# Two heads of lookahead in an attention search, fewer plain products and moved clamps in an attention + MoE kernel

## The chip, the cores and the metric

The kernel runs on one core of one Trainium2 chip. The metric is device microseconds of that core for one execution; the time of a kernel is the median of its runs. The profile shows one further execution.

## What is computed

```python
def reference(q, k, v, moe_*, moe2_*):             # B, H, S, D = 2, 8, 576, 64
    scores = matmul(q, k^T) / sqrt(D)              # float32 everywhere below
    kth = 32nd largest of each row                 # np.partition
    scores = where(scores >= kth, scores, -1e9)
    attn = softmax(scores)                         # sum + 1e-9 in the divisor
    x = (attn @ v) -> (1152 tokens, 512)
    x = ((x @ w_a) * (x @ w_b)) @ w_out            # MoE 1, 512 -> 1536 -> 512, weights float64
    p = domain_probs / (sum + 1e-9)                # MoE 2, 4 experts, 512 -> 1024 -> 512
    return sum_e p[:, e] * (relu(x @ w1[e]) @ w2[e])
```

## The kernel before

Every product is made in two parts, high and low (fp32r), by three passes: the high part is a copy to fp32r (ACT), the low part a subtraction (`split_sb`, L294 and L295, POOL or DVE). The exceptions are "plain" fp32 products: the scores of the (head, batch) pairs in `PLAIN`, which are all (h, 0), and group 0's product with v ("native").

The 1152 tokens are 9 tiles of 128, in three groups of 3 tiles; group 0 takes tiles 3 to 5, which lie in both batches. For each group come the attention of 8 heads x 3 tiles, MoE 1 (`pa`, `pb`, `px`), and MoE 2 (`ph`, `po`).

*Group 0's attention* (called stage 1 below): head by head, `prep(h)` loads q and k (`load_qk`) and splits them; `scores` makes a tile's scores on TensorE (PE) and ACT copies them to `Sb`; in the same step the scores of that head for groups 1 and 2 are made too and kept in DRAM (`stash`, names `pk`, `keep`). DVE then searches each row for its 32nd largest: four MAX8 and three MATCH_REPLACE8 that depend on each other (`top`, `W`, L210 and L212), so the scheduler interleaves two tiles. POOL (group 0) or DVE makes `nm`, ACT the masked exponential in two passes (`Ex`, L218 and L219), PE transposes it (`PT`, `PL`), ACT copies it (`Ph`). `finish(h)`, called in the step after the head's last tile, is the product with v (`pO`), and for every second head the scaling `rs`, `rb`, `pR`, `xf` (L244 to L269), then the split `x`.

*Decode stage*: w_a, w_b and w_out are 18 units of 128 x 1024 numbers in float64. Each is loaded (`wide`, 2 x 512 KB), decoded to float32 (ACT L315, a clamp on POOL L317, ACT L322, two DVE operations L324 and L325 per half), stored to DRAM for the later groups (`da`, `db`, `do`) and split. The first three units are gated by the exponentials and the searches of the last three tiles of group 0 (`GATE`), the others by the last one. Group 0's MoE 1 products follow the units.

*After that* group 0's MoE 2 runs with the attention of group 1 among it, then group 1's MoE with group 2's attention, then group 2's MoE. The order of steps is set by a table of paces, and a scheduler then orders instructions on each engine; each engine runs its own in order.

Buffers in rings: `Sb` 9 (shared with `keep`), `gh` 8, `big` 7, `w` 5, `wraw` 3, `ps_s` 2.

Of the kernel before, what the change touches and what calls it, by code (L numbers as in the profile page):

```python
# [9 lines left out]
F32 = mybir.dt.float32  # L10
R32 = mybir.dt.float32r
# [9 lines left out]
P = 128  # L21
# [8 lines left out]
NB2 = S // P + 1  # L30
N0 = H * GROUPS[0]

NX, NW, NH, NR, NB = 5, 5, 8, 3, 7
NWK, NS, NE, NV = 2, 9, 2, 3
# [17 lines left out]
WC = 256  # L52
# [3 lines left out]
def f32(ap):  # L56
    return ap.bitcast(F32)
# [3 lines left out]
def kernel_body(ctx, tc, qs, ks, vs, wa, wb, wo, dp, w1, w2, out):  # L61
# [43 lines left out]
    kept = {}  # L105
    parts = [[(b, t - b * (S // P)) for b in range(B) if b * S < (t + 1) * P and (b + 1) * S > t * P] for t in range(NT // P)]

    def load_qk(h):
        for b in range(B):
            n = f"{h}_{b}"  # L110
            sl = slice(b * NB2, (b + 1) * NB2)
            kr = sb.tile([P, 4 * WC], F32, tag="big", name=f"kr{n}", bufs=NB)[:, :S]
            qr = sb.tile([P, 2 * MT], F32, tag="gh", name=f"qr{n}", bufs=NH)[:, :NB2 * P].rearrange("p (t c) -> p t c", t=NB2)
# [31 lines left out]
    def attention_steps(g):  # L145
        tpg = GROUPS[g]
        gt = tpg * P
        bt = batches(g)
        native = g in NATIVE
        st = {}  # L150

        def prep(h):
            n = f"{g}_{h}"
            V = {}
            if h % 2 == 0:
                st["sums"] = at.tile([P, MG, 2, 1], F32, tag="sums", name=f"sums{n}")
                st["x"] = at.tile([P, MT], F32, tag="xf", name=f"xf{n}")[:, :gt]
            PL = ps_t.tile([P, 512], F32, tag="PL", name=f"PL{n}")
            Pe = at.tile([P, MT], R32, tag="Pe", name=f"Pe{n}")
            Ph = at.tile([P, 4, MT], R32, tag="Ph", name=f"Ph{n}")  # L160
            Pl = None
            if g == 0:
                load_qk(h)
            if native:
                for b, _, _ in bt:
                    V[b] = at.tile([P, KC, D], F32, tag="V2", name=f"V2{n}_{b}", bufs=NV)
                    nc.sync.dma_start(V[b], vs[b, h])
                Ph, Pe = f32(Ph), f32(Pe)
            else:
                for b, _, _ in bt:  # L170
                    vr = at.tile([P, KC, D], F32, tag="vraw", name=f"vraw{n}_{b}", bufs=1)
                    nc.sync.dma_start(vr, vs[b, h])
                    V2 = at.tile([P, KC, 2 * D], R32, tag="V2", name=f"V2{n}_{b}", bufs=NV)
                    o = D * (h % 2)
                    nc.scalar.activation(V2[:, :, o:o + D], vr, AF.Copy)
# [9 lines left out]
                st["S", i] = S1  # L185

        def scores(h, t):
            if g:
                return st.pop(("S", h * tpg + t))
# [6 lines left out]
            for i in range(1, NG):  # L196
                stash(i, h, t)
            return Sb

        def one_tile(h, t):  # L200


            n = f"{g}_{h}_{t}"
            V, Ph, Pl, Pe, PL, sums, _ = st[h]
            Sb = scores(h, t)
            top = at.tile([P, 32], F32, tag="top", name=f"top{n}")
            W = at.tile([P, S], F32, tag="W", name=f"W{n}", bufs=NWK)
            src = Sb
            for r in range(4):
                last["max", g, h * tpg + t] = nc.vector.max(top[:, 8 * r:8 * r + 8], src).ins  # L210
# [17 lines left out]
                nc.vector.tensor_tensor(Pl[:, :, cols], PT, f32(Ph[:, :, cols]), op=ALU.subtract)  # L228

        def close(h):  # L230
            V, Ph, Pl, Pe, PL, _, _ = st[h]
            nc.scalar.activation(Pe[:64, :gt], PL[:64, :gt], AF.Copy)
            if not native:
                nc.vector.tensor_tensor(Pe[64:, :gt], PL[:64, :gt], f32(Pe[:64, :gt]), op=ALU.subtract)

        def finish(h):
            n = f"{g}_{h}"
            V, Ph, Pl, Pe, PL, sums, xf = st.pop(h)
            late = h == H - 1
            if h % 2:  # L240
# [55 lines left out]


    nload = [0]
    scratch = {}

    def decode(raw, src, n):

        half = 2 * WC
        words = src.bitcast(U32).rearrange("p (n t) -> p n t", t=2)
        gate = GATE[min(len(scratch), len(GATE) - 1)]
        r = raw.bitcast(U32)
        wide = []
        with tc.issue_after(last["exp", 0, gate]):  # L310
# [73 lines left out]
    def moe_steps(g):  # L384
# [159 lines left out]
```

## Time and profile before

| | |
|---|---|
| runs | 922.59, 946.72, 939.25 us; median 939.25 |
| profiled execution | 923.0 us, span 921.2 us, 1.8 us around it |
| mean granted clock of TensorE | 0.970 |
| busy | PE 848.6 us (92%), PEld 744.8, DVE 608.4 (66%), ACT 523.3 (57%), POOL 467.8 (51%) |
| HBM traffic | 141.75 MB, mean 154 GB/s |

The busy shares are means over stages with different limits: PE is nearly full from some 340 us to the end and has gaps before that, while DVE is nearly full from some 160 to 340 us and again from some 480 to 600 us, and four tenths busy or less after that.

### The profile page before, as it was taken

Reading aid. Unit: us, or ns where it says so; the run is one execution under the profiler, and the core shown is the slowest. Engines: PE = TensorE matmul, PEld = TensorE weight load, DVE = VectorE, ACT = ScalarE, POOL = GpSimd, SP = SyncE. Lnnn points to the kernel's source line nnn. Section 1 sums busy time; section 2 is a strip of 40 time slices with the busy share of each in tenths; the row PEclk is TensorE's granted clock in tenths of the full one; section 3 lists DMA queues with packets and bytes.
Section 4 is the critical chain, followed back from the end, with each engine's and each line's share of the span. In section 5 each row is a group of like instructions: output and inputs, shape, how many; then the busy total and the mean of one; then the engine's idle time right before and its main releaser. Section 6 shows DMA issues by size and latency. Waiting matters only on the chain.

```text
span 921.2 us, 12500 instructions
## 1 busy us (share of the span) xinstructions
PE 848.6 (92%) x4332; PEld 744.8 (81%) x4332; DVE 608.4 (66%) x1171; ACT 523.3 (57%) x948; POOL 467.8 (51%) x265
## 2 busy tenths in 40 slices
PE   7988979567777999999999998999999999999997
PEld 5655545357677889999999998999989999899997
DVE  5679587999999997588589999932123222423332
ACT  5776767678777766455567776553333444343330
POOL 4321100579889875545657575455553535422330
PEclk9999988779998999999999999999999999999999
DMA  9645426488765654444455442324334442433420
GB/s 258 197 163 182 147 90 217 132 254 259 239 236 192 205 185 135 140 160 127 152 172 170 140 153 84 115 95 134 128 124 150 136 135 95 153 121 119 139 85 35
DMA packets 50304, 141.75 MB, mean 154 GB/s; under 512 B 5824, under 2 KB 9920, under 8 KB 50240
## 3 DMA queue, kind: packets, MB, share of 16 engines
q1 hardware_dynamic: 50240, 140.94, 47.0%
q8 instruction: 34, 0.56, 0.2%
q14 instruction: 30, 0.25, 0.1%
HBM read 114.97 MB, written 25.95 MB: 153 GB/s over the span
## 4 chain that ended last, share of the span: by engine, by line
PE 62%; DVE 10%; issue 2%; DMA 2%; ACT 0%; DVEq 0%; SPq 0%; ACTq 0%
PE po L451 21%; PE ph L381 20%; PE pb L381 5%; PE pa L381 5%; PE px L420 5%; DVE top L210 2%; DVE W L212 2%; PE PT L223 2%; DVE x L295 1%; PE pO L259 1%; PE pO L258 1%; DVE wraw0o L325 1%; DVE Pl L228 1%; DMA do<-wraw0o 1%; DMA da<-wraw0a 0%
## 5 line engine op out<-in xcount | busy, mean ns | idle before, releaser
L210 DVE MAX8 top<-W 128x8 f32<-128x576 f32 x216 | 158.9, 750 | 1.3
L438 DVE SCALAR_TENSOR_TENSOR h<-ph,h 128x384 fp32r<-128x384 f32 x96 | 52.8, 552 | 141.2 <-ACT h L437 141.1
L437 ACT ACTIVATE h<-ph 128x384 fp32r<-128x384 f32 x96 | 46.6, 489 | 117.9 <-PE ph L381 117.9
L212 DVE MATCH_REPLACE8 W<-top,W 128x576 f32<-128x576 f32 x144 | 106.8, 742 | 0.1
L451 PE MATMUL po<-w1d,h 128*128 128x512 f32 x288 | 71.0, 393 | 2.9 <-DVE xf L269 1.6
L381 PE MATMUL ph<-x,w0u 128*128 128x384 f32 x384 | 72.8, 338 | 0.3 <-DVE x L295 0.3
L381 PE MATMUL ph<-x,w1u 128*128 128x384 f32 x384 | 72.7, 337 | 0.0
L451 PE MATMUL po<-w0d,h 128*128 128x512 f32 x288 | 71.0, 394 | 0.0
L381 PE MATMUL ph<-x,w2u 128*128 128x384 f32 x384 | 70.9, 335 | 0.2 <-DVE x L295 0.2
L451 PE MATMUL po<-w2d,h 128*128 128x512 f32 x288 | 69.9, 392 | 0.0
L223 PE MATMUL PT<-ident,Ex 128*128 128x128 f32 x288 | 48.1, 290 | 23.1 <-ACT Ex L219 21.2
L381 PEld LDWEIGHTS ph<-x,w2u 128*128 128x128 f32 x384 | 67.5, 188 | 2.4 <-DVE x L295 0.5
L381 PEld LDWEIGHTS ph<-x,w0u 128*128 128x128 f32 x384 | 67.2, 188 | 2.3 <-DVE x L295 0.6
L381 PEld LDWEIGHTS ph<-x,w1u 128*128 128x128 f32 x384 | 67.4, 188 | 1.8
L210 DVE MAX8 top<-Sb 128x8 f32<-128x576 f32 x72 | 54.1, 752 | 20.7 <-ACT Ex L218 12.5
L218 ACT ACTIVATE Ex<-Sb,top 128x576 f32<-128x576 f32 x72 | 55.9, 776 | 20.2 <-DVE top L210 19.6
L451 PEld LDWEIGHTS po<-w1d,h 128*128 128x128 f32 x288 | 53.4, 188 | 13.4 <-issue 2.0
L223 PEld LDWEIGHTS PT<-ident,Ex 128*128 128x128 f32 x288 | 36.0, 147 | 34.1 <-ACT Ex L219 25.5
L451 PEld LDWEIGHTS po<-w2d,h 128*128 128x128 f32 x288 | 53.6, 188 | 10.3 <-ACT h L437 0.2
L451 PEld LDWEIGHTS po<-w0d,h 128*128 128x128 f32 x288 | 53.1, 188 | 10.0
L219 ACT ACTIVATE Ex<-Ex,nm 128x576 f32<-128x576 f32 x72 | 55.9, 777 | 7.9 <-DVE nm L215 3.8
L295 POOL TENSOR_TENSOR w1d<-wraw1d,w1d 128x1024 fp32r<-128x1024 f32 x16 | 38.7, 2424 | 38.1 <-ACT w1d L294 38.1
(140 smaller groups left out, 1976.1 us busy)
## 6 DMA issues: line engine op xcount, KB each, us to landing
k<-keep SPq DMA_DIRECT2D x48, 288.0 KB, 3.4
Sb<-k SPq DMA_DIRECT2D x48, 288.0 KB, 3.2
wraw0u<-in_w SPq DMA_DIRECT2D x16, 512.0 KB, 4.1
wraw0d<-in_w SPq DMA_DIRECT2D x16, 512.0 KB, 3.2
wraw1u<-in_w SPq DMA_DIRECT2D x16, 512.0 KB, 3.2
wraw1d<-in_w SPq DMA_DIRECT2D x16, 512.0 KB, 3.2
wraw2u<-in_w SPq DMA_DIRECT2D x16, 512.0 KB, 3.2
wraw2d<-in_w SPq DMA_DIRECT2D x16, 512.0 KB, 3.3
```

The lines of the kernel that those rows point to most:

```text
L210: last["max", g, h * tpg + t] = nc.vector.max(top[:, 8 * r:8 * r + 8], src).ins
L212: nc.vector.match_replace(W, top[:, 8 * r:8 * r + 8], src, LOW)
L218: nc.scalar.activation(Ex, Sb, AF.Prelu, bias=top[:, 31:32], scale=-1.0, alpha=KEEP)
L219: last["exp", g, h * tpg + t] = nc.scalar.activation(Ex, Ex, AF.Exp, bias=nm, scale=-1.0 / (KEEP * math.sqrt(D)), accum_out=sums[:, t, h % ...
L223: nc.tensor.transpose(PT[:, c, :], Ex[:, c * P:(c + 1) * P], ident)
L228: nc.vector.tensor_tensor(Pl[:, :, cols], PT, f32(Ph[:, :, cols]), op=ALU.subtract)
L295: eng.tensor_tensor(dst[:, 1], src, f32(dst[:, 0]), op=ALU.subtract)
L381: nc.tensor.matmul(ps, w[:, a].rearrange("p (c f) -> p c f", c=4)[:, c, col:col + P], xs[c][:, b], start=c == 0 and i == 0, stop=c == k - ...
L420: nc.tensor.matmul(p[:, :gt], w[:, a, o:o + P], ab[:, b], start=f == 0 and i == 0, stop=f == 5 and i == 2)
L437: nc.scalar.activation(ht[:, 0], p[:, :gt], AF.Relu)
L438: nc.vector.scalar_tensor_tensor(ht[:, 1], p[:, :gt], 0.0, f32(ht[:, 0]), op0=ALU.max, op1=ALU.subtract)
L451: nc.tensor.matmul(p, hs[f][:, a, t * P:(t + 1) * P], us[f // 2][:, b, (f % 2) * 512:(f % 2) * 512 + 512], start=hf == 0 and f == 0 and i ...
```

## The change

- **Plain products**: only (0, 0) stays plain. The other 15 pairs are split; for heads 1 to 7 both high parts are made by POOL copies (`CAST`), where ACT made them before. The q and k parts lie in other rings (`gh`, `big`, and a cycle of seven places for `kk`).
- **Order in stage 1**: loads three heads ahead, split and scores two heads ahead (`AHEAD`); `finish(h - 1)` and the `stash` of a tile come after the tile's own search is written. In the order that results, a pair's `xf` on DVE stands several search operations later.
- **Gate**: the first search operation of group 1's first six tiles is issued after the last decoding operation written by then (`NGATE`).
- **Clamps**: the first three units' clamp stays on POOL, the other 15 are two DVE operations each.
- **Smaller moves**: one of MoE 2's two x splits on DVE goes to POOL (`X2_DVE`), and every third low part of group 0's `h` is made by an extra ACT Relu and a POOL subtraction in place of a DVE operation (`H_POOL`).

```diff
-PLAIN = [(h, 0) for h in range(H)]
+PLAIN = [(0, 0)]
+QK_ACT = 1
+LOADS = 3
+AHEAD = 2
-GATE = (N0 - 3, N0 - 2, N0 - 1)
+CLAMP_POOL = range(3)
+GATE = (-3, -2) + (-1,) * 20
-X2_DVE = 2
+X2_DVE = 1
+H_POOL = 3
+NGATE = 6
...
+    def split_qk(h):
+        for b in range(B):
...
+            kr, qr = raw_qk[h, b]
+            A = sb.tile([P, 4 * WC], R32, tag="big", name=f"qa{n}", bufs=NB)[:, :NB2 * P].rearrange("p (t c) -> p t c", t=NB2)
+            i = nkk[0] % (NW + 2)
+            nkk[0] += 1
+            if i < NW:
+                kk = sb.tile([P, 2, 4 * WC], R32, tag="w", name=f"kk{n}", bufs=NW)
...
+            if h < QK_ACT:
+                nc.scalar.activation(A, qr, AF.Copy)
+                nc.scalar.activation(kk[:, 0], kr, AF.Copy)
+            else:
+                nc.gpsimd.tensor_copy(A, qr)
+                nc.gpsimd.tensor_copy(kk[:, 0], kr)
             nc.gpsimd.tensor_tensor(A[64:], qr[64:], f32(A[64:]), op=ALU.subtract)
+            nc.gpsimd.tensor_tensor(kk[:, 1], kr, f32(kk[:, 0]), op=ALU.subtract)
...
+                with ExitStack() as order:
+                    if r == 0 and g == 1 and h * tpg + t < NGATE and "decode" in last:
+                        order.enter_context(tc.issue_after(last["decode"]))
+                    last["max", g, h * tpg + t] = nc.vector.max(top[:, 8 * r:8 * r + 8], src).ins
...
+                    elif t == 0:
+                        for j in range(0 if h == 0 else LOADS, LOADS + 1):
+                            if h + j < H:
+                                load_qk(h + j)
+                        if h == 0:
+                            for j in range(AHEAD):
+                                split_qk(j)
+                                for u in range(tpg):
+                                    scores(j, u)
+                        if h + AHEAD < H:
+                            split_qk(h + AHEAD)
+                    if g == 0 and h + AHEAD < H:
+                        scores(h + AHEAD, t)
+                    if t == 0:
+                        prep(h)
                     one_tile(h, t)
                     if h and t == 0:
                         finish(h - 1)
+                    if g == 0:
+                        for u in range(1, NG):
+                            stash(u, h, t)
...
-        nc.gpsimd.tensor_scalar(raw, raw, -F64_TOP, F64_TOP, op0=ALU.max, op1=ALU.min)
+        if k in CLAMP_POOL:
+            nc.gpsimd.tensor_scalar(raw, raw, -F64_TOP, F64_TOP, op0=ALU.max, op1=ALU.min)
...
+                if k not in CLAMP_POOL:
+                    nc.vector.tensor_scalar(raw[:, hs], raw[:, hs], -F64_TOP, F64_TOP, op0=ALU.max, op1=ALU.min)
...
+                    if g == 0 and H_POOL and nh[0] % H_POOL == 0:
+                        hf32 = sb.tile([P, MT], F32, tag="a", name=f"hf{n}")[:, :gt]
+                        nc.scalar.activation(hf32, p[:, :gt], AF.Relu)
+                        nc.gpsimd.tensor_tensor(ht[:, 1], hf32, f32(ht[:, 0]), op=ALU.subtract)
```

On DVE, at the end of the first pair of heads in stage 1 (names are group, head, tile; `rs`, `xf` belong to the pair of heads 0 and 1), before:

```order
L244 TENSOR_SCALAR rs0_1_520<-sums0_0_81 128x6
L210 MAX top0_2_0_499<-W0_2_0_500 128x8
L245 RECIPROCAL rs0_1_520<-rs0_1_520 128x6
L269 TENSOR_TENSOR xf0_0_82<-pR0_1_525,xf0_0_82 128x384
L210 MAX top0_2_1_576<-Sb0_2_1_545 128x8
L212 MATCH_REPLACE W0_2_1_577<-top0_2_1_576,Sb0_2_1_545 128x576
```

and after:

```order
L253 MAX top0_2_0_613<-W0_2_0_614 128x8
L290 RECIPROCAL rs0_1_634<-rs0_1_634 128x6
L253 MAX top0_2_1_694<-W0_2_1_695 128x8
L255 MATCH_REPLACE W0_2_0_614<-top0_2_0_613,W0_2_0_614 128x576
L255 MATCH_REPLACE W0_2_1_695<-top0_2_1_694,W0_2_1_695 128x576
L253 MAX top0_2_0_613<-W0_2_0_614 128x8
L253 MAX top0_2_1_694<-W0_2_1_695 128x8
L255 MATCH_REPLACE W0_2_1_695<-top0_2_1_694,W0_2_1_695 128x576
L253 MAX top0_2_1_694<-W0_2_1_695 128x8
L314 TENSOR_TENSOR xf0_0_211<-pR0_1_639,xf0_0_211 128x384
L253 MAX top0_2_2_746<-Sb0_2_2_314 128x8
```

Seven search operations of the next head's first two tiles now stand between the reciprocal and `xf`, where none stood.

On PE, early in stage 1 (`pS` are scores for the search, `pk` scores to be kept, `PT` a tile's transposes), before:

```order
L132 MATMUL pS0_0_2_1_209<-kk0_1_97,qa0_1_94 128x288 x2
L132 MATMUL pk2_0_1_1_177<-kk0_1_97,qa0_1_94 128x288 x2
L132 MATMUL pk1_0_2_0_214<-kr0_0_86,qr0_0_87 128x288
L132 MATMUL pk1_0_2_1_217<-kr0_0_86,qr0_0_87 128x288
L132 MATMUL pS0_1_0_0_287<-kr1_0_268,qr1_0_269 128x288
L132 MATMUL pS0_1_0_1_290<-kr1_0_268,qr1_0_269 128x288
L223 MATMUL PT0_0_0_145<-ident_75,Ex0_0_0_142 128x128 x4
L225 MATMUL PL0_0_83<-ident_75,Ex0_0_0_142 64x128
L132 MATMUL pk2_0_2_0_223<-kk0_1_97,qa0_1_94 128x288 x2
L132 MATMUL pk2_0_2_1_227<-kk0_1_97,qa0_1_94 128x288 x2
```

and after:

```order
L268 MATMUL PL0_0_212<-ident_75,Ex0_0_0_230 64x128
L176 MATMUL pS0_1_1_0_168<-kk1_0_147,qa1_0_146 128x288 x2
L176 MATMUL pS0_1_1_1_174<-kk1_0_147,qa1_0_146 128x288 x2
L176 MATMUL pS0_1_1_0_168<-kk1_1_153,qa1_1_152 128x288 x2
L176 MATMUL pS0_1_1_1_174<-kk1_1_153,qa1_1_152 128x288 x2
L266 MATMUL PT0_0_1_287<-ident_75,Ex0_0_1_284 128x128 x4
L268 MATMUL PL0_0_212<-ident_75,Ex0_0_1_284 64x128
L176 MATMUL pS0_1_2_0_181<-kk1_1_153,qa1_1_152 128x288 x2
L176 MATMUL pS0_1_2_1_185<-kk1_1_153,qa1_1_152 128x288 x2
L299 MATMUL pO0_0_432<-Ph0_0_214,V20_0_0_215 64x192 x4
L176 MATMUL pS0_2_0_0_202<-kk2_0_190,qa2_0_189 128x288 x2
```

The scores of heads 1 and 2 now stand among head 0's transposes and ahead of most of head 0's kept scores.

On DVE, where group 0's search ends and decoding begins (`t0a`, `wraw0a` are decoding operations; `top1`, `W1` group 1's search), before:

```order
L212 MATCH_REPLACE W1_0_0_1939<-top1_0_0_1938,W1_0_0_1939 128x576
L212 MATCH_REPLACE W1_0_1_2213<-top1_0_1_2212,W1_0_1_2213 128x576
L246 COPY rb0_7_1599<-rs0_7_1598 128x384
L210 MAX top1_0_0_1938<-W1_0_0_1939 128x8
L210 MAX top1_0_1_2212<-W1_0_1_2213 128x8
L324 SCALAR_TENSOR_TENSOR t0a0_0_1631<-wraw0a0_1623,t0a0_0_1631 128x512
L215 TENSOR_SCALAR nm1_0_0_1947<-top1_0_0_1938 128x1
L212 MATCH_REPLACE W1_0_1_2213<-top1_0_1_2212,W1_0_1_2213 128x576
L325 SCALAR_TENSOR_TENSOR wraw0a0_1623<-wide0a0_0_1624,t0a0_0_1631 128x512
L210 MAX top1_0_2_2448<-Sb1_2_1934 128x8
```

and after:

```order
L396 SCALAR_TENSOR_TENSOR t0b0_0_1764<-wraw0b0_1756,t0b0_0_1764 128x512
L314 TENSOR_TENSOR xf0_6_1398<-pR0_7_1715,xf0_6_1398 128x384
L397 SCALAR_TENSOR_TENSOR wraw0b0_1756<-wide0b0_0_1757,t0b0_0_1764 128x512
L356 TENSOR_TENSOR x0_7_1732<-xf0_6_1398,x0_7_1732 128x384
L396 SCALAR_TENSOR_TENSOR t0b0_1_1768<-wraw0b0_1756,t0b0_1_1768 128x512
L396 SCALAR_TENSOR_TENSOR t0a1_0_1785<-wraw0a1_1777,t0a1_0_1785 128x512
L397 SCALAR_TENSOR_TENSOR wraw0b0_1756<-wide0b0_1_1760,t0b0_1_1768 128x512
L395 TENSOR_SCALAR wraw0b1_1798<-wraw0b1_1798 128x512
L397 SCALAR_TENSOR_TENSOR wraw0a1_1777<-wide0a1_0_1778,t0a1_0_1785 128x512
L395 TENSOR_SCALAR wraw0b1_1798<-wraw0b1_1798 128x512
L396 SCALAR_TENSOR_TENSOR t0a1_1_1789<-wraw0a1_1777,t0a1_1_1789 128x512
L397 SCALAR_TENSOR_TENSOR wraw0a1_1777<-wide0a1_1_1781,t0a1_1_1789 128x512
```

Group 1's search operations are gone from this place (the first stands some 30 rows further down), and two clamps (L395) stand per unit.

## Rows read from the trace of the kernel before

**Rows 1.** Cores: span and mean granted clock of TensorE.

```profile
core 0: 921.2 us, clock 0.970
```

**Rows 2.** Timeline of DVE in stage 1: start, us, operation, idle time before.

```profile
9.35 0.75 DVE L210 MAX8 top<-Sb 128x8 f32<-128x576 f32 x1
...
61.66 0.76 DVE L210 MAX8 top<-Sb 128x8 f32<-128x576 f32 x1 [2.23 <-ACT Sb L195]
...
99.17 0.56 DVE L269 TENSOR_TENSOR xf<-pR,xf 128x384 f32<-128x384 f32 x1 [4.90 <-ACT xf L264]
102.45 0.76 DVE L210 MAX8 top<-Sb 128x8 f32<-128x576 f32 x1 [2.73 <-ACT Sb L195]
...
175.35 1.41 DVE L210 MAX8 top<-W 128x8 f32<-128x576 f32 x2
```

**Rows 3.** Waits of DVE from 0 to 172 us: total us, times, longest.

```profile
DVE top L210 <- ACT Ex L218: 12.5, 6, 4.1
```

**Rows 4.** Timeline of PE where the stages begin: MoE 1 of group 0.

```profile
187.94 1.01 PE L381 MATMUL pa<-x,w0a 128*128 128x384 f32 x2
```

**Rows 5.** Timeline of PE: MoE 2 of group 0 begins.

```profile
320.19 2.62 PE L381 MATMUL ph<-x,w0u 128*128 128x384 f32 x14
```

**Rows 6.** Timeline of PE: group 1's MoE begins.

```profile
469.92 2.26 PE L381 MATMUL pa<-x,w1a 128*128 128x384 f32 x12
```

**Rows 7.** Windows: busy us (count) of PE, PEld, DVE, ACT, POOL, then clock, DMA share, GB/s.

```profile
20.00:40.00 20.00, 20.00 (x61) 13.54 (x61) 13.69 (x28) 14.10 (x36) 7.50 (x8) 1.00 0.63 207
200.00:220.00 20.00, 15.97 (x90) 14.46 (x88) 19.94 (x41) 17.27 (x32) 20.00 (x9) 1.00 0.85 275
...
340.00:360.00 20.00, 20.00 (x105) 18.12 (x104) 17.07 (x38) 10.36 (x18) 12.45 (x6) 1.00 0.48 156
```

**Rows 8.** The chain of waits in the decode stage: start, us, what.

```profile
309.73 5.25 DMA do<-wraw0o
```

**Rows 9.** Lines by form, DVE, 188 to 320 us: busy us, mean ns of one.

```profile
L210 DVE MAX8 top<-Sb 128x8 f32<-128x576 f32 x14 | 10.5, 750 | 0.0
```

**Rows 10.** Lines by form, POOL: busy us, mean ns, idle before.

```profile
L295 POOL TENSOR_TENSOR w0d<-wraw0d,w0d 128x1024 fp32r<-128x1024 f32 x16 | 38.7, 2424 | 32.5 <-ACT w0d L294 32.5
...
L317 POOL TENSOR_SCALAR wraw0a<-wraw0a 128x1024 f32<-128x1024 f32 x6 | 21.8, 3634 | 4.1 <-ACT wraw0a L315 4.0
...
L295 POOL TENSOR_TENSOR kk<-kr,kk 128x576 fp32r<-128x576 f32 x8 | 11.3, 1415 | 17.8 <-ACT kk L294 17.1 <-POOL qa L123 0.7
...
L246 POOL COPY rb<-rs 128x384 f32<-128x384 f32 x9 | 4.6, 508 | 2.1 <-DMA vraw<-in_v 2.1
```

**Rows 11.** Lines by form, DVE: the same columns.

```profile
L438 DVE SCALAR_TENSOR_TENSOR h<-ph,h 128x384 fp32r<-128x384 f32 x96 | 52.8, 552 | 141.2 <-ACT h L437 141.1
...
L324 DVE SCALAR_TENSOR_TENSOR t0a<-wraw0a,t0a 128x512 uint32<-128x512 uint32 x12 | 8.2, 683 | 0.0
...
L246 DVE COPY rb<-rs 128x384 f32<-128x384 f32 x3 | 1.0, 348 | 0.0
```

**Rows 12.** Timeline of POOL, 222 to 234 us.

```profile
227.91 2.41 POOL L295 TENSOR_TENSOR w0o<-wraw0o,w0o 128x1024 fp32r<-128x1024 f32 x1
```

**Rows 13.** Timeline of DVE, 225 to 233 us.

```profile
228.16 3.20 DVE L244 TENSOR_SCALAR rs<-sums 128x6 f32<-128x6 f32 x1
```

**Rows 14.** Timeline of PE, scores in stage 1, split (`kk`) and plain (`kr`).

```profile
29.89 1.16 PE L132 MATMUL pk<-kk,qa 128*128 128x288 f32 x4
...
107.87 0.69 PE L132 MATMUL pk<-kk,qa 128*128 128x288 f32 x4
...
109.63 1.23 PE L132 MATMUL pk<-kr,qr 64*128 64x288 f32 x4
```

**Rows 15.** Lines by form, PE, 320 to 470 us: the same columns.

```profile
L223 PE MATMUL PT<-ident,Ex 128*128 128x128 f32 x52 | 8.3, 274 | 1.2 <-DVE Pl L228 1.2
```

**Rows 16.** Lines by form, PE, 0 to 172 us: the same columns.

```profile
L254 PE MATMUL pO<-Ph,V 128*64 128x192 f32 x112 | 27.7, 404 | 1.8 <-ACT Ph L226 1.8
```

More of the change, by code (lines that the diff above doesn't have):

```diff
@@ L31 @@
 N0 = H * GROUPS[0]
-NX, NW, NH, NR, NB = 5, 5, 8, 3, 7
-NWK, NS, NE, NV = 2, 9, 2, 3
-PLAIN = [(h, 0) for h in range(H)]
-GATE = (N0 - 3, N0 - 2, N0 - 1)
+NX = 5
+NW = 5
+NH = 8
+NR = 3
+NB = 7
+NWK = 2
+NS = 9
+NE = 2
+NV = 3
+PLAIN = [(0, 0)]
[4 more added lines that the diff above has]
+GATE = (-3, -2) + (-1,) * 20
 W_DVE = (0, 0, 2)
-X2_DVE = 2
+X2_DVE = 1
 LOOK = 4
+H_POOL = 3
+NGATE = 6
 PRE = 4
@@ L106, in kernel_body @@
     parts = [[(b, t - b * (S // P)) for b in range(B) if b * S < (t + 1) * P and (b + 1) * S > t * P] for t in range(NT // P)]
+    raw_qk = {}
+    nkk = [0]
     def load_qk(h):
@@ L111, in load_qk @@
             sl = slice(b * NB2, (b + 1) * NB2)
-            kr = sb.tile([P, 4 * WC], F32, tag="big", name=f"kr{n}", bufs=NB)[:, :S]
-            qr = sb.tile([P, 2 * MT], F32, tag="gh", name=f"qr{n}", bufs=NH)[:, :NB2 * P].rearrange("p (t c) -> p t c", t=NB2)
+            raw = lambda c: sb.tile([P, 4 * WC], F32, tag="wraw", name=f"{c}{n}", bufs=NR) if (h, b) in PLAIN else \
+                sb.tile([P, 2 * MT], F32, tag="gh", name=f"{c}{n}", bufs=NH)
+            kr = raw("kr")[:, :S]
+            qr = raw("qr")[:, :NB2 * P].rearrange("p (t c) -> p t c", t=NB2)
             if (h, b) in PLAIN:
@@ L120, in load_qk @@
             nc.sync.dma_start(qr, qs[h, :, sl])
-            A = sb.tile([P, 2 * MT], R32, tag="gh", name=f"qa{n}", bufs=NH)[:, :NB2 * P].rearrange("p (t c) -> p t c", t=NB2)
-            nc.scalar.activation(A, qr, AF.Copy)
+            raw_qk[h, b] = kr, qr
+    def split_qk(h):
+        for b in range(B):
+            if (h, b) in PLAIN:
+                continue
+            n = f"{h}_{b}"
+            kr, qr = raw_qk[h, b]
[4 more added lines that the diff above has]
+                kk = sb.tile([P, 2, 4 * WC], R32, tag="w", name=f"kk{n}", bufs=NW)
+            elif i == NW:
+                kk = at.tile([P, 4, MT], R32, tag="Pl", name=f"kk{n}", bufs=1).rearrange("p (a b) c -> p a (b c)", a=2)
+            else:
+                kk = sb.tile([P, 4, MT], R32, tag="x2f", name=f"kk{n}", bufs=1).rearrange("p (a b) c -> p a (b c)", a=2)
+            kk = kk[:, :, :S]
+            if h < QK_ACT:
+                nc.scalar.activation(A, qr, AF.Copy)
+                nc.scalar.activation(kk[:, 0], kr, AF.Copy)
+            else:
+                nc.gpsimd.tensor_copy(A, qr)
+                nc.gpsimd.tensor_copy(kk[:, 0], kr)
             nc.gpsimd.tensor_tensor(A[64:], qr[64:], f32(A[64:]), op=ALU.subtract)
-            kk = sb.tile([P, 2, 4 * WC], R32, tag="w", name=f"kk{n}", bufs=NW)[:, :, :S]
-            split_sb(kk, kr)
+            nc.gpsimd.tensor_tensor(kk[:, 1], kr, f32(kk[:, 0]), op=ALU.subtract)
             QK[h, b] = (A, (kk[:, 0], kk[:, 1]))
@@ L148, in attention_steps @@
         bt = batches(g)
-        native = g in NATIVE
+        plain = lambda h: g in NATIVE
         st = {}
@@ L161, in prep @@
             Pl = None
-            if g == 0:
-                load_qk(h)
+            native = plain(h)
             if native:
@@ L187, in scores @@
         def scores(h, t):
-            if g:
-                return st.pop(("S", h * tpg + t))
             n = f"{g}_{h}_{t}"
@@ L195, in scores @@
                 nc.scalar.activation(Sb[:, j * SH:(j + 1) * SH], pS[:, :SH], AF.Copy)
-            for i in range(1, NG):
-                stash(i, h, t)
-            return Sb
+            st["S", h * tpg + t] = Sb
         def one_tile(h, t):
             n = f"{g}_{h}_{t}"
+            native = plain(h)
             V, Ph, Pl, Pe, PL, sums, _ = st[h]
-            Sb = scores(h, t)
+            Sb = st.pop(("S", h * tpg + t))
             top = at.tile([P, 32], F32, tag="top", name=f"top{n}")
@@ L230, in close @@
         def close(h):
+            native = plain(h)
             V, Ph, Pl, Pe, PL, _, _ = st[h]
@@ L237, in finish @@
             n = f"{g}_{h}"
+            native = plain(h)
             V, Ph, Pl, Pe, PL, sums, xf = st.pop(h)
@@ L298, in kernel_body @@
     nload = [0]
+    nh = [0]
     scratch = {}
@@ L306, in decode, with behind @@
         words = src.bitcast(U32).rearrange("p (n t) -> p n t", t=2)
-        gate = GATE[min(len(scratch), len(GATE) - 1)]
+        k = len(scratch)
         r = raw.bitcast(U32)
         wide = []
-        with tc.issue_after(last["exp", 0, gate]):
+        def behind(what):
+            gate = ExitStack()
+            if k < len(GATE):
+                gate.enter_context(tc.issue_after(last[what, 0, N0 + GATE[k]]))
+            return gate
+        with behind("exp"):
             for i in range(2):
@@ L320, in decode @@
             t = ps_s.tile([P, half], U32, tag="pS", name=f"t{n}_{i}")
-            with tc.issue_after(last["exp", 0, gate]):
+            with behind("exp"):
                 nc.scalar.activation(t, wide[i][:, :, 0], AF.Copy, scale=0.937 * 2.0 ** -29)
-            with tc.issue_after(last["max", 0, gate]):
+            with behind("max"):
+                if k not in CLAMP_POOL:
+                    nc.vector.tensor_scalar(raw[:, hs], raw[:, hs], -F64_TOP, F64_TOP, op0=ALU.max, op1=ALU.min)
                 nc.vector.scalar_tensor_tensor(t, r[:, hs], 3, t, op0=ALU.logical_shift_left, op1=ALU.bitwise_or)
-                nc.vector.scalar_tensor_tensor(r[:, hs], wide[i][:, :, 1], 0x80000000, t, op0=ALU.bitwise_and, op1=ALU.bitwise_or)
+                found = nc.vector.scalar_tensor_tensor(r[:, hs], wide[i][:, :, 1], 0x80000000, t, op0=ALU.bitwise_and, op1=ALU.bitwise_or)
+            last["decode"] = found.ins
     def load_unit(g, src, key, is_wide):
```

6 lines of the change are left out of this document (3 added, 3 removed).

## The prediction

> **What bounds the kernel now.** I read the cores first: one core, granted clock 0.970, span 921.2 us [rows 1], 923.0 with what lies around it. Then I cut the span where one stage hands over to the next. Group 0's search ends with the last MAX8, at about 176.7 us [rows 2]. The first MoE 1 product starts at 187.9 [rows 4], MoE 2 of group 0 at 320.2 [rows 5], group 1's MoE at 469.9 [rows 6]. So the segments are 176.7, 11.2, 132.3 and 149.7 us, and a remainder of 451.3. The change touches the first, the third and the fourth.
>
> Stage 1 is paced by DVE, but not at DVE's own speed. From the first search of one pair of heads (61.66) to that of the next (102.45) are 40.8 us for six tiles, and in them DVE stands still 4.9 us before `xf` and 2.7 before the next scores [rows 2]. Without these two the six tiles take 33.2 us, 5.5 each. DVE's next instruction is `xf`, and behind it stand searches that could run; PE in its turn has the product with v behind other work. Some waiting for exponentials lies within the 5.5: 12.5 us over the whole stage [rows 3].
>
> In the decode stage PE is not tight: in 200 to 220 us it is busy 16.0 us, DVE and POOL 20 each, and DMA moves 275 GB/s at a share of 0.85 [rows 7]. The chain of waits runs there through DVE's operations in turn and through stores such as `do`, 5.25 us [rows 8]. From 340 us on PE is the bound, busy 20.0 of 20 [rows 7].
>
> **The change part by part.**
>
> *Order in stage 1.* Scores that lie two heads ahead end the wait for them, and seven searches stand where DVE waited for `xf`. From 9.35 us [rows 2] on, 24 tiles x 5.5 = 132 bring T0, the end of group 0's search, to 142. I add 4 for the start: `PT0_0_0` stands ahead of head 1's later scores on PE, and seven casts stand on POOL ahead of the first `nm`. T0 = 146, a gain of 31. Bounds: 138, if the 12.5 us of waiting for exponentials shrink to some 4 and the start costs nothing; 165, if of the gain two thirds are lost to a new wait.
>
> *Splits in place of plain products.* On PE two split products replace one plain one, which the trace records as two. Four split ones took 0.69 us, four recorded plain ones 1.23 [rows 14], so 0.34 against 0.62: PE gains a little, and I count nothing. The price lies on POOL. Per head it has four low parts at some 1.4 [rows 10] (q's are a little longer), `nm` and half an `rb`, together some 7 us, and now four casts of 576 or 640 columns. The trace shows no such cast. The low bound is POOL's COPY, 508 ns for 384 columns, so 0.8 us; the high bound is the clamp, 3634 ns for 1024, so 2.2 [rows 10]. I take 1.5, midway: a copy too, but without the broadcast input. That is 13 us per head, and 15.8 at the high bound, against a search pace of 3 x 5.5 = 16.5. So the two heads of lookahead hide it; without them each head's scores would wait for its split, about 7 us or 50 in all. ACT loses as many copies, which can only help the exponentials; no gain is counted.
>
> *Decode stage.* Fifteen clamps leave POOL: 15 x 3.63 = 54 us [rows 10]. DVE loses most of the 14 searches of group 1 that lay here [rows 9] (I keep two, some 12 us with what follows them) and gains 30 clamps of 512 columns. Their price is not in the trace either: low bound DVE's COPY, 348 ns for 384 columns; high bound a decoding operation, 683 ns [rows 11]. I take 0.4 us, nearer to the copy, which like the clamp reads one operand: 12 us. With 72 decoding operations at 0.68, 49 us, and some 10 of products and small parts, DVE has 83. POOL has 18 low parts at 2.42, three clamps [rows 10], 12 `g` and small parts: 43.6 + 10.9 + 17 = 72. DMA moves 18 units of 1.57 MB (two loads and a store of 512 KB); some 25 MB fall into the stage, 91 us at 275 GB/s [rows 7]. These lie close together, and the last unit must drain, so I take 95 us for 132.3: a gain of 37. Bounds: 80 (two loads are out early and DMA runs faster) and 120 (the clamps wait for POOL, rival A).
>
> *After it.* From 320 to 470 us PE was nearly full. Twelve tiles of group 1 that had been done earlier come here: 52 transposes of 13 tiles took 8.3 us [rows 15], so 0.64 a tile, 8 for twelve, and four heads' products with v at some 1.6, 6 more; a few early tiles of group 2 go, 2 less. So 162, and 12 us are paid back. DVE has 22 tiles x 5.5 = 121, 22 `h` parts at 0.55 [rows 11] = 12, and some 15 of `Pe`, `xf` and `out`: 148, under PE's 162. POOL's extra 10 `h` parts and one x part are some 11 us on an engine that was busy 12.5 of 20 us [rows 7], so they hide; without that room each would delay a product by its 1 us. Bounds 152 and 178.
>
> *The remainder* stays 451: the same products on PE.
>
> The sum: 146 + 11 + 95 + 162 + 451 = 865 of span, 867 for the profiled execution, 56 less than 923.0. That execution lies 1.7% under the median of 939.25; the four known executions (923.0, 922.59, 946.72, 939.25) have a mean of 932.9, 1.1% above it. Not knowing which of them the changed kernel's will be like, I scale by 1.011: 867 becomes **877**.
>
> **A rule against the change.** At 228.16 DVE's `rs`, a TENSOR_SCALAR on six columns, took 3.20 us [rows 13] while POOL ran a low part for 2.41 us from 227.91 [rows 12]. A clamp that meets a POOL operation might be held up likewise.
> The Trainium skill, "SBUF — State Buffer", section "Who interferes with whom", says that VectorE in a two-port mode, `tensor_scalar` among the operations that enter it, and GpSimd share a port pair as an exclusive lock, so that the later one blocks for the whole instruction. The row agrees in kind, though `rs` ended about 1 us after the POOL operation. With no such lock the sum above stands; with it, rival A.
>
> **Rivals.**
>
> *A: the clamps wait for POOL.* POOL is busy through most of the stage, so a clamp waits on average half a low part, 1.2 us: 30 x 1.2 = 36, DVE has 119 in place of 83, and the stage takes some 120 in place of 95. The time is 892, scaled **902**. For it: the 3.20. Against it: with 54 us of clamps gone POOL has gaps.
>
> *B: PE paces stage 1 at its slow rate.* At 29.9 us four split products took 1.16 us, at 107.9 only 0.69 [rows 14], while PE was busy 20.0 of 20 in 20 to 40 us and the granted clock read 1.00 [rows 7]. At the slow rate a head's 40 split products take 11.6 us, three tiles' transposes 3.3, the products with v, 27.7 us for seven heads at both rates [rows 16], some 7, `PL` and `pR` 2: 24. If that rate held, T0 were 9 + 8 x 24 = 201, 55 later than forecast: 922, scaled **932**, no change. Against it: with DVE's stops gone PE has fewer pauses, and the fast rate came in the old order too.
>
> *C, the slower side: POOL's casts pace stage 1.* POOL runs in order, and PE's scores wait for its splits with transposes queued behind them. To be 2% slower than the median the time must reach 958, 948 before scaling: T0 at 227, 27.2 us per head, 27.2 - 7 = 20.2 for four casts, 5.05 each. Per column that is over twice the dearest POOL row. At 5.5 us a cast T0 is 9 + 8 x 29 = 241 and the time 962, scaled **973**.
>
> *D: DVE's debt.* Group 1's postponed search ends late, PE runs dry ahead of group 1's MoE, and DVE's 148 grow by the waits for transposes to some 165, with 11 to drain: 10 to 15 us more, scaled **890**.
>
> **How the numbers follow.** The forecast gets 0.55 (by itself 852 to 890), D 0.15, A 0.15, B 0.08, C 0.03, and 0.04 goes to what I don't see, most of it near no change. The range reaches from 848 (T0 138, decode stage 85) to 908, which takes in D and A; B and C stay out. A measurement of this kernel can tell about 2% from no change: under 920.5 is faster, which holds for the forecast, D and A: 0.85. Within 2%: 0.10 (B and half of the unseen). Slower: 0.05.
>
> **What would show it.** The last MAX8 of group 0 near 146 us, with little idle time ahead of `xf`; POOL casts between 0.8 and 2.2 us; group 0's MoE 2 near 252 us and group 1's MoE near 414. A shows as clamps on DVE far above 0.7 us, B as split products at 0.29 us each past 60 us, C as a full POOL in stage 1 with PE waiting for `qa` and `kk`, D as PE waiting for `x` ahead of 414. The prediction fails if T0 stays above 165 or the decode stage above 120.

## The result, and the profile after

The changed kernel takes 865.85 us (median of 4 runs, 864.12 to 868.47) against 930.92 for the kernel before on the same chip; the ratio is 0.9389, interval 0.9346 to 0.9432. The prediction was 877 us, range 848 to 908. Some runs of the kernel before lie near 945 us; the ratios here and below leave disturbed runs out.

The marks of the stages come first, on PE: MoE 1 of group 0 [rows 4], MoE 2 of group 0 [rows 5], and group 1's MoE in earnest [rows 6] (two early products of it stand at 397 us among the last `po`).

```profile
156.36 0.61 PE L454 MATMUL pa<-x,w0a 128*128 128x384 f32 x2
...
250.38 1.55 PE L454 MATMUL ph<-x,w0u 128*128 128x384 f32 x8
...
413.91 0.77 PE L454 MATMUL pa<-x,w1a 128*128 128x384 f32 x3
```

The account below goes by such marks; for group 1 it takes the first product of its MoE 2, since its MoE 1 starts among other work.

| from | to | before | after | gain |
|---|---|---|---|---|
| 0 | first `pa` of group 0 | 187.9 | 156.4 | 31.6 |
| that | first `ph` of group 0 | 132.3 | 94.0 | 38.2 |
| that | first `ph` of group 1 | 241.5 | 251.7 | -10.3 |
| that | end of span | 359.5 | 360.2 | -0.6 |
| | span | 921.2 | 862.3 | 58.9 |

Next the windows of the stages, with the columns of [rows 7]. First the kernel before, stage 1 and decode stage:

```profile
0.00:176.70 176.70, 146.95 (x594) 94.78 (x595) 131.12 (x269) 119.50 (x280) 44.41 (x56) 0.92 0.55 176
188.00:320.20 132.20, 104.47 (x533) 96.07 (x533) 131.12 (x259) 100.15 (x176) 119.47 (x56) 0.91 0.71 233
```

The changed kernel, stage 1, decode stage, and what follows to 414 us:

```profile
0.00:146.00 146.00, 113.43 (x579) 86.09 (x579) 126.00 (x256) 102.02 (x257) 78.88 (x95) 0.92 0.64 218
156.40:250.40 94.00, 84.00 (x444) 78.76 (x444) 91.32 (x161) 75.23 (x129) 62.54 (x35) 0.96 0.81 290
250.40:413.90 163.50, 162.69 (x882) 146.98 (x881) 160.75 (x344) 112.93 (x202) 100.15 (x59) 1.00 0.47 157
```

Group 0's search ends earlier in the kernel before than the prediction says. The two MAX8 at 175.35 [rows 2] belong to group 1. The last pair's `rs`, which needs the exponentials of all of group 0, starts beside them at 175.28, and the last MAX8 of group 0 is that of 171.00:

```profile
171.00 0.74 DVE L210 MAX8 top<-W 128x8 f32<-128x576 f32 x1
...
175.28 0.80 DVE L244 TENSOR_SCALAR rs<-sums 128x6 f32<-128x6 f32 x1
```

In the changed kernel:

```profile
145.27 0.76 DVE L253 MAX8 top<-W 128x8 f32<-128x576 f32 x1
149.45 0.17 DVE L289 TENSOR_SCALAR rs<-sums 128x6 f32<-128x6 f32 x1 [3.42 <-ACT Ex L262]
```

So the search's end moves from 171.7 to 146.0 and `rs` from 175.3 to 149.4, 26 us. The other 6 of the 31.6 us lie between `rs` and the first `pa`: 12.7 us before, 6.9 after. They come from the gate, which keeps group 1's search out of this place as well: the two changed kernels below that have no gate take 14.0 us there, all that have it 6.9 to 8.2.

The first window above therefore holds 5 us of group 1's search. Up to 171.7 us DVE is busy 126.2, as much as after, and stands still 45.5 us in place of 20.0; PE is busy 143.0 in place of 113.4, 30 us less. In the decode stage POOL fell from 119 to 63 us, but DVE is busy 91 of 94, so it has no room left. Behind it PE and DVE are both full.

The waits of DVE in stage 1 answer to [rows 3]. The 12.5 us for exponentials are down to 4.8, and the waits ahead of `xf`, of which one alone took 4.9 in [rows 2], from 14.2 to 1.9 in all. Before:

```profile
DVE xf L269 <- PE pR L249: 9.3, 2, 5.4
DVE xf L269 <- ACT xf L264: 4.9, 1, 4.9
```

After:

```profile
DVE top L253 <- ACT Sb L236: 7.9, 2, 7.7
DVE rs L289 <- ACT Ex L262: 7.0, 2, 3.6
DVE top L253 <- ACT Ex L261: 4.8, 4, 2.6
DVE xf L314 <- ACT Ex L261: 1.4, 1, 1.4
DVE xf L314 <- ACT xf L309: 0.5, 1, 0.5
```

The 7.7 of the first row is the start. POOL's casts, by form (columns of [rows 10]):

```profile
L166 POOL CAST qa<-qr 128x640 fp32r<-128x640 f32 x14 | 10.1, 719 | 10.7 <-PE pk L176 9.6 <-POOL qa L168 1.0
L167 POOL CAST kk<-kr 128x576 fp32r<-128x576 f32 x14 | 9.3, 666 | 0.1
```

DVE's clamps, by line: least, median and longest, in ns:

```profile
L395 DVE TENSOR_SCALAR wraw0o<-wraw0o x12: 411/420/2368, 176.8 to 232.7; 128x512 f32<-128x512 f32 x12
L395 DVE TENSOR_SCALAR wraw0b<-wraw0b x10: 410/418/945, 160.8 to 215.6; 128x512 f32<-128x512 f32 x10
L395 DVE TENSOR_SCALAR wraw0a<-wraw0a x8: 414/470/1682, 166.2 to 211.0; 128x512 f32<-128x512 f32 x8
```

Eighteen of the 30 take 0.42 us or less; the sum over all is 21.3 us, 9 more than 30 x 0.41.

### The profile page after: what moved, and what is told of

Its sections match the earlier page's. It is cut to its first block, busy times and chain, and to the rows that moved or that the text cites. A ratio compares the mean times of both kernels' runs of the same rounds, so it can differ in the third digit from the quotient of the medians.

```text
span 862.3 us, 12595 instructions
## 1 busy us (share of the span) xinstructions
PE 810.9 (94%) x4332; PEld 732.6 (85%) x4332; DVE 613.9 (71%) x1188; ACT 514.1 (60%) x944; POOL 466.5 (54%) x305
## 5 line engine op out<-in xcount | busy, mean ns | idle before, releaser
L518 DVE SCALAR_TENSOR_TENSOR h<-ph,h 128x384 fp32r<-128x384 f32 x86 | 47.1, 551 | 106.6 <-ACT h L510 106.6
L531 PE MATMUL po<-w0d,h 128*128 128x512 f32 x288 | 75.2, 398 | 0.0
L454 PE MATMUL ph<-x,w0u 128*128 128x384 f32 x384 | 74.9, 340 | 0.1
L531 PE MATMUL po<-w1d,h 128*128 128x512 f32 x288 | 72.8, 394 | 0.0
L531 PEld LDWEIGHTS po<-w2d,h 128*128 128x128 f32 x288 | 53.6, 188 | 10.3 <-ACT h L510 0.2
L269 ACT ACTIVATE Ph<-PT 128x512 fp32r<-128x512 f32 (+1 forms) x72 | 43.1, 599 | 19.3 <-PE PT L266 19.1
```

The source lines that it names most:

```text
L269: nc.scalar.activation(Ph[:, :, cols], PT, AF.Copy)
L454: nc.tensor.matmul(ps, w[:, a].rearrange("p (c f) -> p c f", c=4)[:, c, col:col + P], xs[c][:, b], start=c == 0 and i == 0, stop=c == k - ...
L531: nc.tensor.matmul(p, hs[f][:, a, t * P:(t + 1) * P], us[f // 2][:, b, (f % 2) * 512:(f % 2) * 512 + 512], start=hf == 0 and f == 0 and i ...
```

## The experiments

Twelve kernels. Each is read by its time, by the stage marks of its profile, and where needed by who is full in the stage. Such marks vary between kernels that share a stage unedited, one profile each: the start of `rs` by up to 4.4 us (147.7 to 152.1 in the changed kernel and six others), the decode stage by 3 (94.0 to 97.1 in six), the stretch from the first `ph` of group 0 to that of group 1 by 6 (251.5 to 257.1 in seven). In the diffs a minus is the kernel that the experiment starts from.

### The lookahead taken out

```diff
-LOADS = 3
-AHEAD = 2
+LOADS = 1
+AHEAD = 0
```

> The changed kernel with the lookahead taken out: a head's loads, splits and scores stand in that head's own steps again (loads one head ahead); all else stays, the splits of 15 pairs too. Theory 1 (the order made the gain of stage 1, the splits counted nothing): group 0's search ends near 175 us in place of 146, the casts and low parts of a head (about 5 us) now stand ahead of its scores, and the time is 890 to 905. Theory 2 (the gain of stage 1 came from PE, whose busy time there fell from 147 to 113 us as plain products went): most of the gain stays, the search ends before 155 and the time is below 877.

899.67 us, ratio 0.974 (0.971 to 0.977). The search ends at 174.4 us and `rs` stands at 179.4, 4.1 later than in the kernel before; the first `pa` is at 187.6, where the kernel before has it (187.9), only because the gate shortens the way there. The decode stage stays short, 97.1. Without the lookahead the splits bring nothing. Theory 1 holds; DVE's waits in stage 1 are back, though `finish` is called where the changed kernel calls it (in the kernel before, too, it comes after the search of the next head's first tile):

```profile
DVE xf L314 <- PE pR L294: 14.1, 2, 7.2
DVE top L253 <- ACT Sb L236: 13.0, 4, 7.9
DVE xf L314 <- ACT xf L309: 6.5, 1, 6.5
```

### The splits alone, in the kernel before

```diff
-PLAIN = [(h, 0) for h in range(H)]
+PLAIN = [(0, 0)]
```

> The kernel before with one part of the change alone: all pairs but (0, 0) split, by ACT copies and POOL subtractions, in the old order. Theory 1 (order): the splits save PE 0.28 us for each pair of products but add 1.4 us of ACT and 3 us of POOL per pair ahead of its scores; the search of group 0 ends at 170 to 185, the time is 925 to 935, no change. Theory 2 (PE time): PE loses some 30 us of work in stage 1, the search ends at 155 to 165 and the time is 908 to 918.

917.22 us, ratio 0.9924 (0.9895 to 0.9953). `rs` comes at 169.5, 5.8 earlier, and the first `pa` at 182.4, 5.5 earlier. PE loses 21 us of work (busy 827.9 us in place of 848.6), but DVE then waits for ACT, which here makes the copies (`xf` for ACT's `xf`, 14.4 us). The time and the search's end (about 165 us) both lie at the slow edge of theory 2: PE's work was part of it, and the old order gives most of it away.

### Plain products in the new order

The same pairs (h, 0) plain as before, in the kernel after; their q and k are loaded into the places of the split parts two heads ahead.

```diff
 PLAIN = [(0, 0)]
+LATER = [(h, 0) for h in range(1, H)]
...
+            if (h, b) in LATER:
+                kr = f32(kk[:, 0, :S])
+                qr = f32(kk[:, 1, :NB2 * P]).rearrange("p (t c) -> p t c", t=NB2)
+                nc.sync.dma_start(kr[:64], ks[b, h, :64])
+                nc.sync.dma_start(qr[:64], qs[h, :64, b * NB2:(b + 1) * NB2])
+                QK[h, b] = (qr[:64], (kr[:64],))
+                continue
```

> The changed kernel with the products of (h, 0) plain again for all heads, in the new order with scores two heads ahead; their q and k are loaded into the places of the split parts, two heads ahead, and POOL loses 14 casts and 14 low parts. Theory 1 (the order alone made stage 1's gain, the splits on PE count nothing): group 0's search ends within 5 us of the changed kernel's 146, the time is 860 to 872. Theory 2 (in the new order PE's time counts: with the plain products it has about 147 us of work in stage 1): the search ends at 155 to 168, the time is 875 to 890.

880.28 us, ratio 0.9501 (0.9407 to 0.9595). The first `pa` is at 169.8, 13.4 later than with splits. Theory 2 holds: in the new order PE's time counts. In 0 to 160 us PE is busy 141.8:

```profile
0.00:160.00 160.00, 141.75 (x580) 90.96 (x581) 124.88 (x256) 106.43 (x259) 49.28 (x68) 0.95 0.58 191
```

and DVE waits 21.1 us, in 13 waits, for exponentials (`top` for `Ex`), which come late, as I read it, because PE's full queue delays the transposes that free their buffers:

```profile
DVE top L263 <- ACT Ex L271: 21.1, 13, 7.2
```

So by the start of `rs`, from 175.3 us, the new order alone gives 12.4 us (162.8) and the splits on top of it 13.4 (149.4); the splits in the old order give 5.8 with copies on ACT, and nothing (4.1 later) with casts on POOL and without lookahead. At the first `pa` the order seems to give 18.1, but 5.7 of that is the gate's, which this kernel has too. Each number rests on one profile of each kernel and is good to some 4 us.

Ten of the 13.4 us arise in the first pair of heads, whose `rs` starts at 61.6 in place of 51.6: PE has the scores of three heads to make there and is full from 35 to 62 us, where the changed kernel keeps it busy 23.8 of 27:

```profile
35.00:62.00 27.00, 27.00 (x114) 17.33 (x113) 14.54 (x30) 18.19 (x48) 6.38 (x7) 1.00 0.38 130
```

Of the 21.1 us of waits 12.2 lie in this window. Some of the ten are not PE's work: PE waits 2.4 us, once, for plain operands that are loaded two heads ahead in place of three.

### The high parts of q and k on ACT

```diff
-QK_ACT = 1
+QK_ACT = H
```

> The changed kernel with the high parts of q and k of all heads made by ACT in place of POOL (28 copies, 20 us of ACT at the 0.74 and 0.69 us of the kernel before). Theory 1 (two heads of lookahead hide the splits on either engine): ACT goes from 102 to 122 of 146 us in stage 1, the search of group 0 ends within 4 us of 146, the time is 864 to 872. Theory 2 (exponentials are what the search waits for, and ACT is in turn): each copy delays an exponential, the search ends 8 to 15 us later, the time is 874 to 882.

872.16 us, ratio 0.9444 (0.9396 to 0.9492). The search ends at 148.7 us and `rs` of the last heads starts at 152.3, where the kernels with this stage unedited have it between 147.7 and 152.1, so stage 1 says theory 1; the time, 6 us more, sits at theory 1's upper end. Where the casts are made costs little at most.

### Kept scores first

```diff
+                    if g == 0:
+                        for u in range(1, NG):
+                            stash(u, h, t)
                     if t == 0:
                         prep(h)
                     one_tile(h, t)
                     if h and t == 0:
                         finish(h - 1)
-                    if g == 0:
-                        for u in range(1, NG):
-                            stash(u, h, t)
```

> The changed kernel with the kept scores of a tile (groups 1 and 2) written ahead of that tile's search instead of after it. Theory 1 (what matters is how far ahead the scores lie, not where the kept ones stand): within 4 us, 862 to 870. Theory 2 (kept scores ahead of a tile's transposes hold up the exponentials' chain on PE and ACT): four stalls of 2 to 4 us come back, 874 to 882.

865.90 us, ratio 0.9375 (0.9342 to 0.9407): no difference, theory 1.

### Clamps back on POOL

```diff
-CLAMP_POOL = range(3)
+CLAMP_POOL = range(18)
```

> The changed kernel with all 18 clamps on POOL again (54 us more there, 21 us less on DVE); the gate stays. Theory 1 (the decode stage became shorter because POOL lost the clamps): POOL has 63 + 54 = 117 us in the stage, which then takes 115 to 122 in place of 94, some of it given back because DVE searches in its idle time: 878 to 890. Theory 2 (the gate on group 1's search alone made it shorter): within 5 us, 862 to 872.

892.02 us, ratio 0.9639 (0.9598 to 0.9681). The decode stage takes 118.9 us, and POOL is its bound, 115.9 busy, with DVE at 75:

```profile
159.10:278.00 118.90, 93.56 (x449) 86.32 (x449) 75.02 (x134) 78.06 (x131) 115.86 (x51) 0.87 0.70 232
```

Theory 1 for the mechanism; the time is 2 us above its range, as nearly nothing was given back: DVE's gated search can't use the idle time.

### No gate

```diff
-NGATE = 6
+NGATE = 0
```

> The changed kernel without the gate: group 1's search may start as soon as its scores are there, between decoding operations. Theory 1 (DVE is the bound of the decode stage, busy 91 of 94 us, and searches in it delay the weights while PE waits): 6 to 10 more tiles of 5.5 us are searched in the stage, it takes 120 to 135, and part comes back afterwards because PE and DVE have less to do: 872 to 890. Theory 2 (what DVE does early it needs not do late, and DVE is full from 156 to 414 us either way): within 5 us, 862 to 871.

900.56 us, ratio 0.9745 (0.9704 to 0.9785). Eleven tiles of group 1 start in the decode stage in place of five, and it takes 136.0 us:

```profile
161.70:297.70 136.00, 104.98 (x522) 95.25 (x522) 134.80 (x266) 97.80 (x172) 66.51 (x40) 0.89 0.67 221
```

DVE is full, POOL idle half the time: theory 1's mechanism, 10 us above its range. From `rs` (147.7) to the first `pa` are 14.0 us here in place of 6.9. Of the 42 us that the stage grows, 7 come back up to the first `ph` of group 1 (244.7 in place of 251.7) and 4 after it.

### Neither gate nor moved clamps

```diff
-CLAMP_POOL = range(3)
-NGATE = 6
+CLAMP_POOL = range(18)
+NGATE = 0
```

> The changed kernel without the gate and with all clamps on POOL: the fourth cell beside the changed kernel (both, decode stage 94 us), the gate alone (119) and the clamps alone (136). Theory 1 (either engine by itself keeps the stage long: DVE with searches, POOL with clamps, so each part alone gives little): the stage takes 128 to 138 us and the time is 893 to 903, as without the gate. Theory 2 (the two gains simply add up, 42 for the gate and 25 for the clamps): the stage takes 155 to 165 us and the time is 915 to 930.

893.96 us, ratio 0.9622 (0.9558 to 0.9686); the stage takes 129.7 us, and from `rs` to the first `pa` are 14.0. Theory 1. The four cells, decode stage and time:

| | searches gated | not gated |
|---|---|---|
| clamps on DVE | 94.0 us, 865.9 | 136.0 us, 900.6 |
| clamps on POOL | 118.9 us, 892.0 | 129.7 us, 894.0 |

With no gate the moved clamps cost 6 us of stage, with it they gain 25.

### The clamps moved, in the kernel before

```diff
-        nc.gpsimd.tensor_scalar(raw, raw, -F64_TOP, F64_TOP, op0=ALU.max, op1=ALU.min)
+        k = len(scratch)
+        if k < 3:
+            nc.gpsimd.tensor_scalar(raw, raw, -F64_TOP, F64_TOP, op0=ALU.max, op1=ALU.min)
...
+                if k >= 3:
+                    nc.vector.tensor_scalar(raw[:, hs], raw[:, hs], -F64_TOP, F64_TOP, op0=ALU.max, op1=ALU.min)
```

> The kernel before with 15 of the 18 clamps moved to DVE and nothing else: no gate, old order. Theory 1 (both parts are needed: DVE was full there, 131 of 132 us, so clamps on it take the time that they free on POOL): the stage stays at 125 to 140 us, 925 to 940. Theory 2 (POOL was the bound, the searches give way): the stage falls to 100 to 110, and the time to 900 to 912.

933.19 us, ratio 1.0098 (1.0064 to 1.0133), about 1% slower. POOL falls from 119 to 66 us and the stage stays at 133.1, since DVE is full. Theory 1.

### Each clamp on DVE twice

```diff
+                    nc.vector.tensor_scalar(raw[:, hs], raw[:, hs], -F64_TOP, F64_TOP, op0=ALU.max, op1=ALU.min)
                     nc.vector.tensor_scalar(raw[:, hs], raw[:, hs], -F64_TOP, F64_TOP, op0=ALU.max, op1=ALU.min)
```

> The changed kernel with each of the 30 clamps on DVE made twice, which costs DVE as much again as the change did (21 us, 0.71 each). Theory 1 (DVE bounds the decode stage and the MoE 2 stage behind it has no room left): group 1's MoE and the end come 15 to 22 us later, 881 to 888. Theory 2 (PE and DMA bound the two stages, DVE's busy time is only filled up by searches that could come later): 866 to 873.

889.05 us, ratio 0.9613 (0.957 to 0.9657), 23 us more; the decode stage grows by 22.2 to 116.2. The 60 clamps take 49 us in place of 21, and DVE is busy 24 us more in the stage. Theory 1, 1 us above its range: DVE has no room there, and what it gets to do more makes the stage longer.

```profile
158.00:274.20 116.20, 92.61 (x443) 84.38 (x443) 115.61 (x191) 76.19 (x127) 63.47 (x35) 0.90 0.69 233
```

### All low parts of h on DVE

```diff
-H_POOL = 3
+H_POOL = 0
```

> The changed kernel with all low parts of group 0's h on DVE again (10 x 0.55 = 5.5 us more of DVE between 250 and 414 us, where it is busy 161 of 164 and PE 163). Theory 1 (DVE paces that stage): the end comes 4 to 7 us later, 869 to 873. Theory 2 (PE paces it, DVE only keeps up): within 2 us, 864 to 868.

872.50 us, ratio 0.9391 (0.9343 to 0.9438). The ratio doesn't differ from the changed kernel's; the median is 6.6 us above that of the changed kernel's own runs. In the profiles, 3.2 us of it arise before the first `ph`, where the two programs are the same, and 5.1 between the first `ph` of group 0 and that of group 1 (256.8 against 251.7), about the price of the ten operations. But six other kernels with that stretch unedited have it between 251.5 and 257.1 too, so neither the times nor the profiles settle it. The moved x split (`X2_DVE`) was not run by itself.

### Less on DVE

```diff
-CLAMP_POOL = range(3)
-H_POOL = 3
+CLAMP_POOL = (0, 1, 2, 5, 8, 11, 14)
+H_POOL = 2
```

> The changed kernel with less on DVE: four more units' clamps on POOL (units 5, 8, 11 and 14, 5.7 us off DVE, 14.5 onto POOL, which is busy 63 of 94 us in the decode stage), and every second in place of every third low part of h off DVE (3.3 us). Theory 1 (DVE paces both stages, and PE has 10 us of waiting in the decode stage to give): 857 to 862. Theory 2 (a clamp on POOL delays its unit by more than it frees, or PE paces the rest): 865 to 872.

873.37 us, ratio 0.9404 (0.935 to 0.9457), not better. The decode stage takes 101.6 us against 94.0, with DVE waiting some 12 us for ACT's steps of the decoding in place of 5. Theory 2 for the clamps: DVE is as busy as before (91.3 us), since the 22 clamps left on it take 19.2 us where 30 took 21.3, and it is held up more. So this run does not show what less work on DVE alone would give. I tried no other split, so a better one is not excluded.

## Why the prediction was right, point by point

*Segments.* 146 + 11 + 95 were forecast ahead of the first `ph` and 146 + 10.4 + 94.0 measured; the 12 us paid back afterwards became 13.8 up to the mark that I had named (413.9), and the remainder 448 in place of 451. The profiled span, 865 forecast, is 862.3. That the 11 came out is luck: it was read from 176.7, where group 1's search was already under way. From the true end at 171.7 the kernel before takes 16.2 us to the first `pa`, and the gate, which I counted for the decode stage alone, brought that down to 10.4.

*The scale to the median.* The 1.011, from the spread of the kernel before, was the larger error: four runs of the changed kernel lie within 0.5%, near its profiled one.

*Order in stage 1.* The 146 was right, the gain of 31 and its reason were not. The search's end gained 26 us. I gave all of the gain to the order and wrote that PE "gains a little, and I count nothing". By `rs` the order alone gives some 12 us and the splits on PE some 13 more; the remaining 6 of the 31.6 at the first `pa` are the gate's. With DVE's stalls gone PE was next: plain products keep it at 142 of 160 us. My 146 came out because it was built up from 5.5 us per tile, and not from the wrong 176.7, and because PE, which I had left out, lost enough work to keep up with that pace: with the plain products the same order ends the search at 159.8.

*The casts.* Forecast 1.5 us between 0.8 and 2.2; measured 0.72 and 0.67, under the low end, so the copy that broadcasts was a poor neighbour. Rival C needed 5.05 and is out. The lookahead hides them, as said; without it `rs` comes 30 us later, where I had put 50.

*Decode stage.* POOL was priced at 72 us and measured 63; the stage 95, measured 94.0. But the bound is DVE: 83 forecast, 91 measured, from five tiles in place of two that start there and clamps at 0.71 on average in place of 0.4. My dearest term was DMA's, 91 us, so the 95 came out because DVE's happen to be 91 too. It is DVE, and not DMA or POOL, that I should have named: doubling the clamps made DVE 24 us busier and the stage 22 longer.

*Rival A.* The mechanism is there and its price a quarter of what I gave. The rows show it: a clamp that starts while POOL runs a low part ends 0.3 us after it. DVE:

```profile
193.22 0.75 DVE L253 MAX8 top<-W 128x8 f32<-128x576 f32 x1
...
219.13 0.41 DVE L395 TENSOR_SCALAR wraw0o<-wraw0o 128x512 f32<-128x512 f32 x1
...
220.13 2.23 DVE L395 TENSOR_SCALAR wraw0o<-wraw0o 128x512 f32<-128x512 f32 x1
...
226.87 2.37 DVE L395 TENSOR_SCALAR wraw0o<-wraw0o 128x512 f32<-128x512 f32 x1
```

and POOL:

```profile
192.43 2.52 POOL L356 TENSOR_TENSOR w0o<-wraw0o,w0o 128x1024 fp32r<-128x1024 f32 x1
...
219.72 2.35 POOL L356 TENSOR_TENSOR w0a<-wraw0a,w0a 128x1024 fp32r<-128x1024 f32 x1 [3.79 <-issue]
...
226.57 2.39 POOL L356 TENSOR_TENSOR w0b<-wraw0b,w0b 128x1024 fp32r<-128x1024 f32 x1 [2.09 <-ACT w0b L355]
```

The clamp of 220.13 ends at 222.36, POOL's operation at 222.07; that of 226.87 at 229.24 against 228.96, where the clamp of 219.13, begun while POOL was idle, took 0.41. The MAX8 of 193.22 lies wholly within POOL's operation of 192.43 and took its usual 0.75.
The Trainium skill, "SBUF — State Buffer", section "Who interferes with whom", has this as an exclusive lock of a shared port pair, in which the one that comes later waits for the whole of the other. The trace agrees for the clamps, 0.41 us alone and up to 2.37 behind a POOL operation.
All in all the waits add 9 us to 30 clamps, 0.3 each and not 1.2. POOL is idle a third of the stage after the clamps left, and in five of the 15 units the second clamp follows a first that has already waited; so 18 of the 30 were not held up.

*The gate.* I took it as what frees DVE for decoding, and it carries more than I said: it takes 6 us out ahead of the first `pa`, and without it the moved clamps lose 6 us, with it they gain 25. Moving work off one full engine onto another full one gives nothing.

*Rivals B and D.* Four split products take 0.83 us at 27.8 us and 0.69 at 33.7, so the fast rate came earlier than before, not later. DVE's debt is real: 161 of 163.5 us where I had 148, leaving 3 of the 14 us of room under PE that I counted on; PE still was busy 162.7, so little was lost to it.

## What to carry to other kernels

When two engines are full in one stage, moving work from the first to the second shows nothing until work is taken off the second; test the two edits as four cells, not one at a time. When the stalls of the pacing engine go, name the next engine and price its work too: here a saving on PE that was worth some 6 us in the old order was worth some 13 in the new one, ten of them at the start of the stage. A stage's end must be read from an operation that belongs to it: the last search of a kind was another group's here, which made one stage 5 us too long and the next 5 too short. Work that is pushed out of a stage must be counted where it lands: DVE paid nearly all of it in the next stage, with 3 us to spare.

## What the runs showed of the hardware

A DVE TENSOR_SCALAR of 128x512 from SBUF to SBUF took 0.41 us alone and up to 2.37 beside a POOL operation, while MAX8 at 0.75 was not held up. POOL casts 576 columns of fp32 in 0.67 us, 1.16 ns each, where its copy with a broadcast input took 1.3 and its clamp with two operations 3.5. The seven kernels with the same stage 1 ended it up to 4.4 us apart.
